# Full-height score products, query tiles loaded in pairs, DMA transposes of late x and a fixed order of tasks in a fused attention and SwiGLU kernel

## The chip, the core and the metric

The kernel runs on one core of one Trainium2 chip. The metric is the time on the device, in microseconds (us). Each run is one execution with its own time; one execution of each kernel was also profiled. "Span" is the length of the profiled execution, which lies about 1.7 us under the time of the same run (283.4 against 285.07 for the kernel before).

Engines: PE is TensorE (matrix products), PEld its weight loads, ACT is ScalarE, DVE is VectorE, POOL is GpSimd, SP issues DMAs.

## The reference, cut to what matters

```python
# q, k, v: (4, 8, 768, 64) f32; heads 0, 2, 6 see all earlier keys ("retrieval"),
# heads 1, 3, 4, 5, 7 only the first 4 keys and the last 64 ("sink + window")
scores = q @ k.T / 8                     # per batch and head, 768 x 768
scores = where(mask, scores, -1e9)       # causal, or causal & (sink | window)
a = softmax(scores)
x = (a @ v).transpose(0, 2, 1, 3).reshape(3072, 512)
g, val = x @ w_gate, x @ w_val           # 512 -> 1536
out = (silu(g) * val) @ w_out            # 1536 -> 512, f32
```

The kernel cuts the 3072 rows into 24 query tiles of 128. Two neighbouring tiles of a batch form a pair, 12 pairs in all, counted here from 0. Each pair has its own loads of q, k and v (512 KB each, f32). The three weight matrices (3.1 MB each) are loaded once, between the loads of pairs 1 and 4. A group of tiles, whose x is complete, goes through the gate, value and output products; a group's work is twelve column blocks of gate and value products and then its output products.

## The kernel before

q and k of a pair are cast to f16, transposed on TensorE, and copied from PSUM into one tensor `qkT`. Scores of a head use 64 rows of the array; the two heads of a head pair lie in the upper and lower half.

```python
SIZES = [2, 2, 4, 4, 4, 4, 4]            # query tiles per group
...
def transposes(n, w):                    # w: 0 for q, 1 for k
    tr = buf("tr", [128, 2, 4, 128], FH, "tr")
    for j in range(2):
        for p in range(4):
            nc.tensor.transpose(tr[:, j, p, :],
                hqs[n][:, w, j, p // 2, (p % 2) * 128:(p % 2 + 1) * 128], ident)
...
def scores(t, u, unit):
    sc = scs[t, u] = buf("sc", [128, 2, 4, 128], FP, "sc")
    for n in range(4):
        for s in range(2):               # the half of the rows, and of the PSUM tile
            if n < len(unit[s]):
                h, _, _, kk, vv = unit[s][n]
                nc.tensor.matmul(sc[:, s, n, :], kk,
                    T[s * 64:s * 64 + 64, 0, p, i * 128:(i + 1) * 128])
...
def xtranspose(t):                       # the attention's result, to feed the gates
    tr = buf("tr", [128, 4, 128], FH, "xtr")
    for p in range(4):
        nc.tensor.transpose(tr[:, p, :], xb[:, p].rearrange("p a d -> p (a d)"), ident)
```

A list scheduler with estimated durations orders the tasks while the kernel is built. At run time every engine works through its own list in order; the brackets in the timelines below name what an instruction waited for. An instruction that waits also holds back every later one of its engine.

The softmax here doesn't subtract the row's maximum and nothing guards it: scores larger than these inputs give would overflow.

## Time and profile before

| | kernel before |
|---|---|
| time, median of 3 runs | 285.65 us (284.93 to 286.28) |
| span of the profiled run | 283.4 us |
| PE busy | 261.6 us, 92% |
| copies, casts, masks: DVE, ACT, POOL busy | 161.5, 160.3, 133.7 us |
| end of the loads | about 105 us |

How to read it: PE is the bound as soon as it never waits, which holds from 90 us on (139.97 of the 140 us up to 230 are busy). What can be saved is therefore PE work, and the time that PE loses in the first 90 us. For the second I use one measure throughout. In the built order one can count the PE work that stands ahead of any instruction (0.2158, 0.1092, 0.0558 and 0.0295 us for products of 512, 256, 128 and 65 columns, from distances between starts; warm-up products count as nothing). The start of that instruction in the trace, less the work ahead of it, is the time lost up to there. The lines of the profile are shown in the prediction.

### The profile page before, as it was taken

What the parts mean: (1) busy time and instruction counts of PE and PEld (TensorE: products, weight loads), DVE (VectorE), ACT (ScalarE), POOL (GpSimd) and SP (SyncE); (2) the same over time, 40 slices, a digit from 0 to 9 for tenths busy, and PEclk for the clock granted to TensorE, in tenths of its full rate; (3) what the DMA queues carried; (4) which work ended last, traced back from release to release, by engine and by line L of the source; (5) the groups of instructions that cost most, each with busy time, mean ns of one, the idle gap of its engine ahead of it and who ended that gap; (6) DMA issues with size and microseconds to landing.
All of it is one profiled execution on the core that took longest, in us unless ns stands there. A gap on an engine that the chain in (4) does not pass through costs nothing.

```text
span 283.4 us, 5690 instructions
## 1 busy us (share of the span) xinstructions
PE 261.6 (92%) x2232; PEld 142.3 (50%) x2232; DVE 161.5 (57%) x319; ACT 160.3 (57%) x255; POOL 133.7 (47%) x194
## 2 busy tenths in 40 slices
PE   7358887989996999999999999999999999999994
PEld 6245665556644446454454454554554544444441
DVE  5374775646553667655574566685575564555500
ACT  3566877988954866648539656425526633332311
POOL 5669848876974557827425527408506410000000
PEclk9656999799999999999999999999999999999999
DMA  7999999999999990100000101110011010000022
GB/s 190 255 341 349 327 243 317 345 212 273 267 266 243 255 244 4 38 2 37 37 33 6 39 0 39 38 39 31 10 38 39 1 39 37 37 35 4 37 89 96
DMA packets 61514, 34.96 MB, mean 123 GB/s; under 512 B 26032, under 2 KB 57008, under 8 KB 61488
## 3 DMA queue, kind: packets, MB, share of 16 engines
q1 hardware_dynamic: 61344, 34.48, 45.0%
q8 instruction: 17, 0.28, 0.4%
q10 hardware_dynamic: 144, 0.13, 0.1%
q14 instruction: 9, 0.07, 0.1%
HBM read 28.31 MB, written 6.29 MB: 122 GB/s over the span
## 4 chain that ended last, share of the span: by engine, by line
PE 75%; DMA 13%; SPq 3%; ACT 2%; DVE 2%; issue 2%; POOL 1%; ACTq 0%; POOLq 0%
PE gv L635 39%; PE o_ps L665 18%; DMA raw<-in_k_dram 10%; PE sc L421 6%; PE av L463 5%; PE tr L355 3%; DMA raw<-in_v_dram 2%; PE xtr L480 2%; PE gv L665 2%; SPq L277 2%; SPq L269 1%; DMA raw<-in_moe_w_out_dram 1%; POOL e L454 1%; ACT e L435 1%; ACT hq L172 1%
## 5 line engine op out<-in xcount | busy, mean ns | idle before, releaser
L647 DVE SCALAR_TENSOR_TENSOR sil<-sig,gv 128x512 f32<-128x512 f32 (+1 forms) x84 | 51.1, 609 | 45.8 <-ACT sig L642 45.6
L635 PE MATMUL gv<-xt,wv_sb 128*128 128x512 f16 (+1 forms) x336 | 76.5, 353 | 0.7 <-DVE sil L647 0.7
L642 ACT ACTIVATE sig<-gv 128x512 f32<-128x512 f32 (+1 forms) x84 | 44.6, 538 | 55.9 <-PE gv L635 55.8
L635 PE MATMUL gv<-xt,wg_sb 128*128 128x512 f16 (+1 forms) x336 | 75.2, 352 | 0.0
L454 POOL TENSOR_TENSOR e<-e,m 128x1024 f16<-128x1024 f16 (+1 forms) x42 | 59.7, 1433 | 24.0 <-ACT e L435 23.6
L665 PE MATMUL o_ps<-wo_sb,h 128*128 128x512 f16 x264 | 67.6, 380 | 0.1
L435 ACT ACTIVATE e<-sc 128x1024 f16<-128x1024 f32 x48 | 49.2, 1025 | 23.1 <-PE sc L421 22.7
L654 DVE SCALAR_TENSOR_TENSOR h<-sil,gv 128x512 f16<-128x512 f32 (+1 forms) x84 | 51.2, 611 | 15.7 <-PE gv L635 12.1
L635 PEld LDWEIGHTS <-wg_sb 128*128 128x128 f16 x336 | 31.3, 99 | 26.3 <-issue 0.4
L665 PEld LDWEIGHTS <-h 128*128 128x128 f16 x288 | 27.2, 98 | 29.8 <-issue 0.4
L635 PEld LDWEIGHTS <-wv_sb 128*128 128x128 f16 x336 | 29.2, 99 | 23.8 <-issue 1.2
L454 POOL TENSOR_TENSOR e<-e,diag 128x128 f16<-128x128 f16 x60 | 24.8, 429 | 16.9 <-ACT e L439 11.3
L421 PE MATMUL sc<-qkT 64*128 64x128 f16 x392 | 26.9, 232 | 3.6 <-ACT e L435 2.3
L172 ACT CAST hq<-raw 128x512 f16<-128x512 f32 x44 | 25.9, 624 | 7.7 <-DMA raw<-in_q_dram 3.9
L463 PE MATMUL av<-vt,e 128*128 128x65 f16 x392 | 23.1, 197 | 5.8 <-POOL e L454 2.7
L421 PEld LDWEIGHTS <-qkT 64*128 64x128 f16 x392 | 14.8, 99 | 24.4 <-issue 19.1
L463 PEld LDWEIGHTS <-e 128*128 128x128 f16 x472 | 19.4, 99 | 13.9 <-POOL e L454 4.7
L471 DVE RECIPROCAL rc<-av 128x4 f32<-128x4 f32 x48 | 8.7, 181 | 26.0 <-PE av L463 25.7
L680 ACT COPY o_sb<-o_ps 128x512 f32<-128x512 f32 x22 | 12.9, 587 | 15.0 <-PE o_ps L665 15.0
L472 DVE TENSOR_TENSOR xb<-av,rc 128x256 f16<-128x256 f32 x48 | 20.4, 425 | 1.7
L174 DVE COPY qkT<-tr 128x1024 f16<-128x1024 f16 x14 | 17.1, 1222 | 7.2 <-PE tr L355 7.1
L378 POOL COPY k<-qkT 128x256 f16<-128x256 f16 x16 | 6.4, 397 | 30.7 <-DVE qkT L174 21.4
(50 smaller groups left out, 184.8 us busy)
## 6 DMA issues: line engine op xcount, KB each, us to landing
raw<-in_q_dram SPq DMA_DIRECT2D x12, 512.0 KB, 6.0
raw<-in_k_dram SPq DMA_DIRECT2D x12, 512.0 KB, 6.2
raw<-in_v_dram SPq DMA_DIRECT2D x24, 256.0 KB, 6.1
out_dram<-o_sb SPq DMA_DIRECT2D x23, 256.0 KB, 2.0
raw<-in_moe_w_gate_dram SPq DMA_DIRECT2D x6, 512.0 KB, 9.2
raw<-in_moe_w_val_dram SPq DMA_DIRECT2D x6, 512.0 KB, 8.9
raw<-in_moe_w_out_dram SPq DMA_DIRECT2D x6, 512.0 KB, 6.9
out_dram<-o_sb SPq DMA_DIRECT2D x1, 128.0 KB, 1.7
```

What stands on the lines that cost most here:

```text
L172: nc.scalar.copy(out=dst, in_=src)
L174: ENG[task.way[0]].tensor_copy(out=dst, in_=src)
L421: nc.tensor.matmul(sc[:, s, n, :], kk, T[s * 64:s * 64 + 64, 0, p, i * 128:(i + 1) * 128])
L435: nc.scalar.activation(out=e[:, :, 0:na], in_=sc[:, :, 0:na], func=AF.Exp, scale=scale)
L454: eng.tensor_tensor(out=ev, in0=ev, in1=mm, op=ALU.mult)
L463: nc.tensor.matmul(av[:, n, 0:65], ee, vv, start=(m == 0), stop=(m == len(bl) - 1))
L472: nc.vector.tensor_tensor(out=xbs[t][:, :, odd, :], in0=av[:, :, 0:64], in1=rc.to_broadcast([128, 4, 64]), op=ALU.mult)
L635: nc.tensor.matmul(ps, wsb[:, kk, j * 128:(j + 1) * 128], xt[:, kk, 0:w], start=(kk == 0), stop=(kk == 3))
L642: nc.scalar.activation(out=sg[g, j], in_=gs[g, j], func=AF.Tanh, scale=0.5)
L647: nc.vector.scalar_tensor_tensor(out=sl[g, j], in0=sg.pop((g, j)), scalar=1.0, op0=ALU.add, in1=gs.pop((g, j)), op1=ALU.mult)
L654: nc.vector.scalar_tensor_tensor(out=hs[g, j], in0=sl.pop((g, j)), scalar=0.5, op0=ALU.mult, in1=vs.pop((g, j)), op1=ALU.mult)
L665: nc.tensor.matmul(o_open[g, tt], hs[g, j][:, tt * 128:(tt + 1) * 128], wo_sb[:, j, :], start=(j == 0), stop=(j == NJ - 1))
```

## The change

Its intent is to fill the array's rows in the scores, to load and transpose q as pairs of tiles in a block-diagonal form, to take the transposes of late x off TensorE, and to replace the scheduler by a fixed order with 149 extra warm-up products in the early holes. The diff has 958 lines; this is its core, with cuts.

```diff
+ORDER = ("000403010205061F1G07xy1L1H1I1N1Mxm1O1Q1P08xt1R1J..."   # cut: the order of all tasks
+WAYS = ("0000000000000000000000000000000000000000000000..."       # cut: the engine of each
-    SIZES = [2, 2, 4, 4, 4, 4, 4]
+    SIZES = [4, 4, 4, 4, 4, 4]
+    HALVES = 4                          # column blocks of group 0 done in two halves of 256
+    XBAR = 12                           # tiles from 12 on: x by DMA transposes
...
-    qkT = [const.tile([128, 2, 4, S], FH, name=f"qkT{n}") for n in range(2)]
+    kT = [const.tile([128, 4, S], FH, name=f"kT{n}") for n in range(2)]
+    qT = [const.tile([128, 4, 2, 2, 128], FH, name=f"qT{n}") for n in range(2)]
+            nc.vector.memset(qT[n][0:64, :, 1], 0.0)       # zeros beside each head's q
+            nc.vector.memset(qT[n][64:128, :, 0], 0.0)
...
 def scores(t, u, unit):
+    for p, hh, c, kt in unit[0]:         # both heads of pair p in one product
+        nc.tensor.matmul(
+            sc[c // 4][:, c % 4:c % 4 + len(hh), :], block(t, p, kt),
+            qT[t // 2 % 2][:, p, hh[0]:hh[-1] + 1, :, half])
...
 def xtranspose(t):
+    if t >= XBAR:
+        for p in range(4):
+            nc.sync.dma_start_transpose(
+                out=xts[g][:, p, n * 128:(n + 1) * 128],
+                in_=xb[:, p].rearrange("p a d -> p (a d)"))
+        return
...
 def oevac(g, tt):                        # the last tile of the output
-        nc.scalar.copy(out=o_sb[:, 0:256], in_=o_ps[:, 0:256])
-        nc.vector.tensor_copy(out=o_sb[:, 256:512], in_=o_ps[:, 256:512])
+        nc.scalar.copy(out=o_sb[0:64], in_=o_ps[0:64])
+        nc.vector.tensor_copy(out=o_sb[64:128], in_=o_ps[64:128])
...
     for number in P.order():
+        if number < 3700:
+            P.tasks[number].run()
+        else:
+            warm(number - 3700)          # warm-up products between the tasks
```

The copy of transposed q out of PSUM becomes two copies of 64 partitions, since the two heads of a pair go to different places: one on ACT and one on DVE in nine of the twelve pairs, both on DVE in three.

## The prediction

> **What bounds the kernel now.** I read the busy table first, then the 40 slices, then the engines by stage, then the order of matmuls in time, and last the waits for loads.
>
> ```profile
> PE 261.6 (92%) x2232; PEld 142.3 (50%) x2232; DVE 161.5 (57%) x319; ACT 160.3 (57%) x255; POOL 133.7 (47%) x194
> ...
> PEclk9656999799999999999999999999999999999999
> DMA  7999999999999990100000101110011010000022
> ```
>
> TensorE is the only engine near full. Loads fill the DMA engines for the first 15 slices (some 105 us). The granted clock is low in slices 2 to 4 and in slice 8.
>
> ```profile
> 0.00:30.00 30.00, 19.48 (x195) 15.50 (x196) 16.56 (x38) 16.86 (x21) 21.39 (x42) 0.72 1.06 287
> 30.00:60.00 30.00, 26.52 (x287) 18.16 (x286) 20.00 (x48) 24.63 (x44) 21.93 (x30) 0.94 1.09 294
> 60.00:90.00 30.00, 26.02 (x310) 16.41 (x310) 16.05 (x39) 22.15 (x39) 21.50 (x33) 1.00 1.05 257
> 90.00:230.00 140.00, 139.97 (x1214) 69.87 (x1213) 86.81 (x161) 82.43 (x129) 68.91 (x90) 1.00 0.19 51
> ```
>
> The columns are stretch, length, busy PE, PEld, DVE, ACT, POOL, clock, DMA share, GB/s. From 90 us on TensorE never stops; before that it does. But busy time overstates, since neighbouring matmuls overlap in the record, so I count work by distances between starts in the dense part of the timeline: 0.216 us for a matmul of 512 columns (eight in 1.73), 0.109 for 256, 0.056 for 128 (eight transposes in 0.45), 0.0295 for 65. The scores are special:
>
> ```profile
> 102.18 1.90 PE L635 MATMUL gv<-xt,wg_sb 128*128 128x512 f16 x8
> 104.02 0.40 PE L421 MATMUL sc<-qkT 64*128 64x128 f16 x8
> 104.35 0.20 PE L463 MATMUL av<-vt,e 128*128 128x65 f16 x1
> ```
>
> Eight gate matmuls need 1.73 us, yet the scores start 1.84 after them: 0.11 is lost on entering. Eight score blocks go in pairs, one pair each 0.057, so 0.23; the next product starts after 0.33, so 0.10 is lost on leaving. A visit costs 0.21 us beside its work.
>
> Demand before, by the built order's counts: 768 of 512 columns 165.7, 192 of 256 20.9, 288 transposes 16.1, 472 value products 13.9, 472 score blocks 13.5, and 67 visits to scores 14.1: 244.2 us. Copying out and storing the last tile takes 3.7 (279.7 to 283.4). So 283.4 - 244.2 - 3.7 = 35.5 us are lost, nearly all early. Pair 4 of query tiles, counted from 0, shows why:
>
> ```profile
> 57.38 0.62 ACT L172 CAST hq<-raw 128x512 f16<-128x512 f32 x1 [0.46 <-DMA raw<-in_q_dram]
> 59.26 0.62 ACT L172 CAST hq<-raw 128x512 f16<-128x512 f32 x1 [0.71 <-DMA raw<-in_k_dram]
> ...
> 69.47 0.61 PE L355 MATMUL tr<-ident,hq 128*128 128x128 f16 x8
> ...
> 88.94 0.35 PE L463 MATMUL av<-vt,e 128*128 128x65 f16 x6 [2.13 <-POOL e L454]
> ```
>
> ACT waits for q and k of this pair; its k transposes run at 69.47, when about 40 us of demand are done (35.8 of work, some 20 visits). So 29.5 us were lost by then and 6.0 after it, 2.1 of them in the wait for a GpSimd mask at 88.94.
>
> [...] from 10 to 20 us the clock is 0.50, and eight score blocks that take 0.40 later are recorded with 0.61. [...] a DVE cast of 128x512 issued at 12.82, inside a POOL copy of 1.94 us, took 2.27 us, and 0.43 elsewhere. [...]
>
> **The change part by part.** Scores: 67 visits and 472 half-height blocks (27.6 us) become 196 full-height products of 256 columns (21.4) and 80 of 128 (4.5), since half of each moving operand is zeros. 25.9 instead of 27.6 saves only 1.7; a full unit of eight blocks costs 0.44 both ways.
>
> Late x: 12 tiles lose four PE transposes each, 48 x 0.056 = 2.7 us, and 12 DVE copies of 0.423. In the built order of the change the DMA transposes of a group's last tile stand 6 to 8 us of PE work ahead of the first gate, and all stand behind the input loads.
>
> Group sizes: seven groups become six, the first with halves for 4 of 12 column blocks. In 256-column form a gate pair keeps DVE 0.84 us for 0.87 of PE, in 512-column form 1.37 for 1.73, so the early stage loses a DVE limit. PE demand of the gates is unchanged.
>
> PE demand after: 832 x 0.216 = 179.5 (exact 0.2158), 64 x 0.109 = 7.0, 240 transposes 13.4, values 13.9, scores 25.9: **239.7**, less by 4.5. Extra warm-up products (189 for 40) stand in expected holes of the first 30 us and should keep the clock.
>
> Masks: POOL loses 85.0 us of them (46.8 + 24.8 + 13.4) and keeps some 18: about 4 x 2.13 + 7 x 1.33. It falls to some 70. DVE takes 20 of 0.68 and 13 of about 0.42, 23 casts of 0.43 and 11 output copies of about 0.69 (estimates scaled from rows of the same operation), and rises to about 195. ACT falls to about 143 (21 casts, 11 output copies, 4 weight casts fewer; about 9 us of q and k copies more). None passes TensorE.
>
> New order: this is the main term. The bytes ahead of k of pair 4 are the same (four pairs, all weights, its q), and DMA is full, so it should land near 59.3; a cast of 0.62 makes 59.9. In the changed order only 35.2 us of PE work stand ahead of its transposes (72 transposes, 24 for x, 49 + 15 score products, 97 value products, 64 gates of 256 columns, 64 products of 512). The PE cannot pass this point before 59.9, so at least 59.9 - 35.2 = **24.7** are lost. I choose this as the loss to that point, against 29.5 before: whatever the quicker start wins earlier is taken back by the load. The same test for k of pair 2 (cast at 38.2 before, 15.9 of work ahead) gives 22.9, consistent.
>
> Afterwards I keep 2.5 of the 6.0 lost: mask waits go, stores no longer stand between loads, but DVE gets tighter. Sum of span: 239.7 + 24.7 + 2.5 + 3.7 = 270.6; the timed median stands 2.2 above the profiled span (285.65 against 283.4): **272.8 us**, 4.5% faster.
>
> **The rivals.** (1) VectorE becomes the early bound. Between 10 and 60 us of PE demand it carries about 46 us by the counts, and the 2.27 us cast shows what a collision with GpSimd adds. For: 56 masks and casts move to it. Against: GpSimd's load halves. If it binds, 5 to 8 us more: 278 to 281. (2) The loads do go faster, as buffers come free sooner: slice 6 moved 243 GB/s where neighbours moved over 315, about 2 us of loading. Then 268 to 271. (3) DMA transposes and stores share one in-order queue with two output buffers; a transpose group over some 8 us would hold back gates or stores. No trace line gives their duration. Three late groups at a few us each: about 280. (4) The fixed order stalls every engine where one estimate was wrong, while it also keeps the slow clock: 3 to 5 us, 276 to 278.
>
> **Range and chances.** The low end, 266, needs a loss of 20 to pair 4 and almost none later; the high end, 279, one of rivals 1, 3 or 4 in full. The line for faster by over 2% is 279.9; only two rivals together pass it. So faster 0.88, same 0.10, slower 0.02.
>
> **What would show it.** Right: no 64-row matmuls; score units of eight blocks at 0.44 us without holes at their edges; PE waiting at the q or k transposes of pairs 2 to 4 for loads; the k transposes of pair 4 near 60 us; dense PE from some 65 us; POOL near 70 and DVE near 195 us; clock above 0.8 from 10 to 30 us. Wrong: k of pair 4 landing well before or after 59; PE waits on DVE in the middle; gates of the last three groups waiting on DMA transposes.

Marked cuts are passages that no trace or run of this case shows. The sum came to 239.7 + 24.7 + 2.5 + 3.7 + 2.2 = 272.8 us. That the DVE cast of 2.27 us was held up by the POOL copy running beside it is the reading of that one overlap; the 5 to 8 us of the first rival are an estimate.

## The result, and the profile after

| | before | changed |
|---|---|---|
| time, median of 4 runs | 285.49 us (284.93 to 286.28) | 277.46 us (276.55 to 278.45) |
| span of the profiled run | 283.4 us | 276.7 us |
| ratio | | 0.9717, 95% interval 0.9676 to 0.9759 |

A ratio is the mean time of one kernel's fast runs over that of the other's fast runs of the same rounds, so it is not quite the ratio of the medians quoted. The changed kernel is 2.8% faster. The profiled run of the changed kernel was its slowest of four.

First the page: busy times, then the granted clock and the DMA engines in 40 slices of 6.9 us.

```profile
PE 261.1 (94%) x2073; PEld 152.9 (55%) x2073; DVE 182.0 (66%) x368; ACT 146.5 (53%) x210; POOL 72.9 (26%) x106
...
PEclk9988989999999999999999999999999999999998
DMA  7999999999999994311022121122113021102233
```

ACT and POOL end near the prediction's 143 and 70 us; DVE, at 182, stays 13 us below its 195. The early clock is high (0.94 over the first 30 us, against 0.72), and the loads fill the DMA engines for as long as before (the first 15 slices, some 104 us here and 106 before).

The same stretches as before, columns as in the prediction:

```profile
0.00:30.00 30.00, 25.21 (x332) 22.23 (x333) 19.42 (x55) 18.22 (x24) 16.18 (x37) 0.94 1.02 277
30.00:60.00 30.00, 26.77 (x224) 16.88 (x223) 23.30 (x50) 21.40 (x34) 13.01 (x17) 0.94 1.07 298
60.00:90.00 30.00, 29.46 (x283) 18.59 (x280) 22.86 (x51) 23.39 (x33) 11.09 (x19) 1.00 1.10 252
90.00:230.00 140.00, 138.20 (x1052) 76.73 (x1051) 98.23 (x188) 72.27 (x104) 32.60 (x35) 1.00 0.30 67
```

PE now is dense from 60 us on, where it had 26.02 of 30 us before. In the first 30 us it is busier by 5.7 us, but 149 extra warm-up products of 0.056 us or more are in that. And the last stretch has 1.8 us of holes that the kernel before had not.

Then the timeline, at the places where PE falls behind (here and below, lines between those shown are left out):

```profile
37.87 0.76 DVE L179 CAST hq<-raw 128x512 f16<-128x512 f32 x2 [0.96 <-DMA raw<-in_q_dram]
38.36 0.73 PE L387 MATMUL tr<-ident,hq 128*128 128x128 f16 x8 [1.32 <-DVE hq L179]
...
63.21 0.61 PE L387 MATMUL tr<-ident,hq 128*128 128x128 f16 x8 [0.52 <-DVE qT L179]
...
111.66 1.17 POOL L179 CAST vt<-raw 128x512 f16<-128x512 f32 x2 [4.15 <-DMA raw<-in_v_dram]
112.79 2.12 POOL L495 TENSOR_TENSOR e<-e,m 128x1024 f16<-128x1024 f16 x1
114.97 0.42 PE L504 MATMUL av<-vt,e 128*128 128x65 f16 x8 [1.47 <-POOL e L495]
...
272.14 0.58 ACT L730 COPY o_sb<-gv 64x512 f32<-64x512 f32 x1 [2.00 <-PE gv L720]
272.75 0.69 DVE L731 COPY o_sb<-gv 64x512 f32<-64x512 f32 x1 [9.46 <-ACT o_sb L730]
```

The square brackets give the idle time of the engine before the line and what ended it. At 38.36 us PE waits for a cast of q of pair 2, which waited for its load: 13.7 us of work are ahead, so 24.7 us are lost here already, the loss that the prediction expected only at pair 4. At 63.21, the k transposes of pair 4, 35.2 us of work are ahead and 28.0 are lost, and the wait is not for k but for a DVE copy of q. At 114.97 a value product waits for a mask on POOL that stood behind the cast of a late v load. At the end the two half copies of the last tile run one after the other.

The span fell by 6.7 us: 4.5 us less PE work, 3.1 less lost (35.5 to 32.4), 0.9 more in the end from the first copy of the last tile on (3.7 to 4.6).

### The profile page after: what moved, and what is told of

Read it like the earlier page. It is cut to its first block, busy times and chain, and to the rows that moved or that the text cites. A ratio compares the mean times of both kernels' runs of the same rounds, so it can differ in the third digit from the quotient of the medians.

```text
span 276.7 us, 5346 instructions
## 1 busy us (share of the span) xinstructions
PE 261.1 (94%) x2073; PEld 152.9 (55%) x2073; DVE 182.0 (66%) x368; ACT 146.5 (53%) x210; POOL 72.9 (26%) x106
## 4 chain that ended last, share of the span: by engine, by line
PE 73%; DMA 8%; ACT 6%; SPq 4%; POOL 3%; issue 3%; DVE 2%; POOLq 0%; ACTq 0%; DVEq 0%
PE gv L692 37%; PE o_ps L720 17%; PE sc L470 8%; PE av L504 4%; DMA raw<-in_q_dram 3%; PE tr L387 3%; DMA raw<-in_k_dram 3%; PE gv L720 2%; ACT qT L177 1%; DMA xt<-xb 1%; ACT e L487 1%; SPq L524 1%; POOL e L495 1%; POOL vt L179 1%; SPq L304 1%
## 5 line engine op out<-in xcount | busy, mean ns | idle before, releaser
L487 ACT ACTIVATE e<-sc 128x1024 f16<-128x1024 f32 (+4 forms) x67 | 60.9, 910 | 37.3 <-PE sc L470 37.1
L709 DVE SCALAR_TENSOR_TENSOR h<-sil,gv 128x512 f16<-128x512 f32 (+1 forms) x76 | 49.3, 657 | 15.3 <-PE gv L692 13.7
L692 PEld LDWEIGHTS <-wg_sb 128*128 128x128 f16 x304 | 28.9, 99 | 27.3 <-issue 1.4
L470 PE MATMUL sc<-qT,kT 128*128 128x256 f16 (+1 forms) x228 | 35.9, 262 | 0.8 <-DVE kT L179 0.4
L495 POOL TENSOR_TENSOR e<-e,m 128x640 f16<-128x640 f16 (+1 forms) x11 | 18.2, 1662 | 42.6 <-ACT e L487 42.4
L470 PEld LDWEIGHTS <-kT 128*128 128x128 f16 x228 | 20.9, 99 | 12.1 <-issue 1.1
L179 POOL CAST vt<-raw 128x512 f16<-128x512 f32 x24 | 15.3, 659 | 41.5 <-DMA raw<-in_v_dram 37.4
L495 DVE TENSOR_TENSOR e<-e,m 128x1024 f16<-128x1024 f16 (+1 forms) x33 | 20.8, 631 | 7.6 <-ACT e L487 7.3
L387 PE MATMUL tr<-ident,hq 128*128 128x128 f16 x192 | 15.3, 223 | 3.8 <-DVE hq L179 3.0
L177 ACT CAST hq<-raw 128x512 f16<-128x512 f32 x23 | 14.0, 618 | 9.0 <-DMA raw<-in_k_dram 6.0
L387 PEld LDWEIGHTS <-hq 128*128 128x128 f16 x192 | 12.6, 100 | 8.4 <-DVE hq L179 3.6
L418 POOL COPY k<-kT 128x256 f16<-128x256 f16 x16 | 7.0, 435 | 37.9 <-DVE kT L179 24.8
```

The source lines that it names most:

```text
L179: ENG[task.way[0]].tensor_copy(out=dst, in_=src)
L387: nc.tensor.transpose(tr[:, j, p, :], hqs[n][:, w, j, p // 2, (p % 2) * 128:(p % 2 + 1) * 128], ident)
L470: nc.tensor.matmul(sc[c // 4][:, c % 4:c % 4 + len(hh), :], block(t, p, kt), qT[t // 2 % 2][:, p, hh[0]:hh[-1] + 1, :, half])
L487: nc.scalar.activation(out=e[:, 0:n], in_=whole_sc.pop((t, u))[:, 0:n], func=AF.Exp, scale=scale)
L495: ENG[task().way[0]].tensor_tensor(out=ev, in0=ev, in1=mm, op=ALU.mult)
L692: nc.tensor.matmul(ps, wsb[:, kk, j * 128:(j + 1) * 128], xt[:, kk, c[0]:c[1]], start=(kk == 0), stop=(kk == 3))
```

## The experiments

Most experiments alter only the lists. They are written as edits of the fixed order: ("after", a, b) puts the tasks b behind task a in the common order, from which each engine's list follows; ("way", n, t) gives task t to another engine of its choices. In the names, `cq2.0` is the first half cast of q of pair 2, `tr2.0` and `tr2.1` its q and k transposes, `evq`, `evk` the copies out of PSUM, `cx` a cast of v, `wc` the cast of a weight load, `gate0.5`, `tanh0.5`, `stt1 0.5`, `vals0.5`, `stt2 0.5` the steps of column block 5 in group 0. Built orders were checked for every dependence and every reuse of a buffer. Line numbers of the experiments are shifted against the changed kernel.

The runs, with the changed kernel itself as an anchor in the third call:

| call | run | median us (range) | ratio to before (95%) |
|---|---|---|---|
| 1 | half-height scores | 278.05 (277.42 to 279.60) | 0.9736 (0.9701 to 0.9770) |
| 1 | late x on TensorE | 281.29 (280.69 to 281.85) | 0.9842 (0.9811 to 0.9874) |
| 1 | few warm-up products | 276.88 (276.29 to 278.27) | 0.9695 (0.9660 to 0.9730) |
| 1 | transposes later | 278.63 (278.37 to 279.41) | 0.9756 (0.9722 to 0.9789) |
| 2 | weight casts on GpSimd | 278.40 (277.22 to 280.80) | 0.9732 (0.9687 to 0.9777) |
| 2 | mask first | 276.87 (275.46 to 277.44) | 0.9659 (0.9623 to 0.9694) |
| 2 | one copy of the last tile | 277.22 (276.58 to 278.30) | 0.9682 (0.9650 to 0.9715) |
| 2 | four edits | 275.80 (275.17 to 275.94) | 0.9627 (0.9597 to 0.9656) |
| 3 | changed kernel again | 277.53 (277.13 to 277.99) | 0.9683 (0.9643 to 0.9723) |
| 3 | both limits | 277.62 (277.13 to 279.08) | 0.9691 (0.9655 to 0.9728) |
| 3 | combined | 275.50 (275.16 to 276.68) | 0.9617 (0.9580 to 0.9655) |
| 4 | refined, five fast runs | 274.17 (273.72 to 276.98) | 0.9585 (0.9533 to 0.9636) |

A call is one set of runs taken together; the calls ran on different chips (6 for call 1, 5 for call 2, 11 for calls 3 and 4). For call 4 the kernel before was run only once more, and its other eleven runs are those of call 3. The kernel before gave medians of 285.13, 286.39, 286.85 and 286.87 in the four calls. The changed kernel's ratio came out as 0.9717 in the first set and as 0.9683 in call 3, with nearly the same median (277.46 and 277.53): it is the kernel before that scatters. So I compare medians of the edited kernels with 277.5 and take nothing under 1 us as shown by times alone. Calls 1 and 2 had no run of the changed kernel itself, so their comparison goes across chips. The mechanism is read from the traces, by the loss at fixed places:

| lost, us, up to | before | changed | later | GpSimd casts | both limits | combined | refined |
|---|---|---|---|---|---|---|---|
| k transposes of pair 2 | 24.0 | 24.5 | 24.8 | 26.0 | 22.4 | 22.1 | 21.6 |
| k transposes of pair 4 | 29.9 | 27.1 | 28.0 | 28.3 | 26.6 | 26.2 | 25.3 |
| copy of the last tile | 35.5 | 31.5 | 32.4 | 32.1 | 31.0 | 30.9 | 28.9 |

"Changed" is here the trace of the anchor run, whose time of 277.53 is the median; in the slower profiled run shown above the three numbers are 26.0, 28.0 and 32.4. A difference of 1 to 1.5 us between two traces of the same kernel is thus normal. The traces of mask first and one copy, whose early lists are those of the changed kernel, lie between these two: 24.9 and 24.9 at pair 2, 27.0 and 27.4 at pair 4.

### What the parts are worth: scores, DMA transposes, warm-up products

**Half-height scores.** The changed kernel with the old form; the two heads lie in different halves of the PSUM tile, as before. Query tiles with five key blocks use units of 7 and 2 score blocks in place of 8 and 1, so that no half has more than four.

```diff
-    for p, hh, c, kt in unit[0]:
-        nc.tensor.matmul(sc[c // 4][:, c % 4:c % 4 + len(hh), :], block(t, p, kt),
-                         qT[t // 2 % 2][:, p, hh[0]:hh[-1] + 1, :, half])
+    for n in range(len(rows[1])):
+        for s_ in range(2):              # rows[s_]: the blocks of one half of the rows
+            if n < len(rows[s_]):
+                p, kt = rows[s_][n]
+                part = slice(s_ * 64, s_ * 64 + 64)
+                nc.tensor.matmul(sc[s_][:, n if s_ else n + 4 - len(rows[0]), :],
+                                 block(t, p, kt)[part], qT[t // 2 % 2][part, p, s_, :, half])
```

> The changed kernel with the old form of the scores: each head's block is a product over 64 rows of the array[...]; order, copies, masks and loads stay as in the changed kernel. Theory (the demand account of the prediction): 472 half-height blocks and 68 visits cost 13.5 + 14.3 = 27.8 us where the full-height form costs 25.9, all of it on TensorE; so some 1.9 us more than the changed kernel (277.5), about 279.4, ratio to the kernel before near 0.978, and the 64-row units show gaps of some 0.1 us at both edges again. Rival (the form is the main part of the gain[...]): 283 or more, ratio over 0.99.

Measured: 278.05 us, 0.5 above the changed kernel; correct. From its timeline:

```profile
175.76 1.03 PE L768 MATMUL o_ps<-wo_sb,h 128*128 128x512 f16 x4
176.72 0.40 PE L507 MATMUL sc<-qT,kT 64*128 64x128 f16 x8
177.05 1.90 PE L740 MATMUL gv<-xt,wv_sb 128*128 128x512 f16 x8
```

Four products of 0.216 us end at 176.62, the scores start 0.10 later, and the next product comes after 0.33 us where eight half-height blocks need 0.23. So the edges are back, 0.20 us a unit of eight. But 0.10 + 0.33 is 0.43 us for eight blocks, and the full-height form takes four times 0.109, 0.44: for a full unit nothing is gained, only for the units with fewer blocks. Units that fill the two halves unevenly pay more on leaving (0.13 to 0.21 us in this trace). Summed over the 67 visits that is 27.8 us against 25.9 for the full-height form, a difference of 2.0, as the expectation had it; the times show only 0.5, within their scatter, and the trace loses some 1.6 us less elsewhere than the anchor's (0.9 of that is a wait of the anchor that comes and goes; see the end). The form of the scores is a small part of the gain; the rival of 283 or more is out.

**Late x on TensorE.** XBAR is 24, and the copies of late x are placed in DVE's list behind the next PE tasks.

```diff
-    XBAR = 12
+    XBAR = 24
+EDITS = [("after", "stt1 2.1.0", "xe12"), ("after", "sc14.0", "xe13"), ...]   # cut
```

> The changed kernel with x of the 12 late tiles transposed on TensorE and copied out by VectorE, as for the early tiles, in place of the DMA transposes. Theory: 48 transposes of 0.056 us come back to a TensorE that is full from some 65 us on, +2.7 us, less the one visible wait of 0.6 us for a DMA transpose: some 2 us more than the changed kernel, about 279.6, ratio near 0.979. Rival (the DMA transposes cost more than the trace shows, since they stand in the queue with the stores, or VectorE has holes that the copies fit badly): no difference or a little faster for the first half, ratio 0.972 or less; over 1 us beyond the theory's size (281 or more) if VectorE's 12 more copies of 0.42 us hold back the gates.

Measured: 281.29 us, 3.8 more, and beyond the expected 2. The demand rose by the counted 2.7 us; the rest is lost time (32.8 at the last copy against 31.5). The table of waits of PE shows two that are new; columns are the waiting group, the one waited for, us in total, times, and the longest:

```profile
PE xtr L584 <- DVE kT L233: 0.9, 1, 0.9
...
PE tr L441 <- DVE xt L589: 0.5, 1, 0.5
```

Transposes of x and of q and k share a single PSUM buffer, so x on TensorE also queues for it; the two waits stand at 177 and 187 us. Taking late x off TensorE is thus worth 3.8 us, more than the 2.7 that the products cost. This is the largest single part that I could isolate. The new order, the group sizes and the new division of masks and casts among the engines were not tested one by one; by the times, about 4 of the 8.0 us between the kernels remain with them together.

**Few warm-up products.** 131 of the 149 extra products are left out.

```diff
-        else:
+        elif number in (3718,):          # the first extra set, 18 products
             warm(number - 3700)
```

> The changed kernel without 131 of its 149 extra warm-up products (those placed in holes of the first 30 us; the 40 at the start and the first 18 stay). Theory: the loss of the early stage is set by when q and k of pairs 2 to 4 land, and TensorE waits for them at either clock, so the time stays within 1 us of the changed kernel (276.5 to 278.5), although the granted clock falls in slices 2 to 4. Rival (the quicker start is the clock's doing): with the clock near 0.5 to 0.65 in the first 30 us as in the kernel before, some 15 us of TensorE work take up to twice as long and the time rises by 3 us or more, 280.5 and over.

Measured: 276.88 us, 0.6 less than the changed kernel, although the granted clock read 0.7, 0.7 and 0.5 in slices 3 to 5, counted from 1 (14 to 34 us). The prediction was that the warm-up products "should keep the clock". They do (0.9 or more in each of these slices of the anchor), and it is worth nothing here, as PE waits at either clock: before the transposes of q and k it stood 2.1 us in this trace and 3.4 in the anchor's, before the scores 2.8 and 1.4. Something else was unexpected. Two traces in stretches of 1 us, of the kernel with all warm-up products (it is the one with one copy of the last tile):

```profile
15.00:16.00 1.00, 0.19 (x4) 0.02 (x1) 0.15 (x1) 0.35 (x2) 0.00 (x0) 1.00 0.95 155
16.00:17.00 1.00, 0.67 (x12) 0.57 (x13) 0.79 (x3) 0.98 (x2) 0.32 (x1) 1.00 0.58 127
```

and of the kernel with few:

```profile
15.00:16.00 1.00, 0.62 (x8) 0.45 (x9) 0.65 (x3) 0.97 (x3) 0.29 (x1) 1.00 1.42 246
16.00:17.00 1.00, 0.42 (x12) 0.33 (x10) 0.21 (x1) 0.98 (x2) 1.00 (x3) 1.00 1.00 295
```

The last number is GB/s. With all the warm-up products the loads dip, and k of pair 1 is cast from 15.85 us on, against 14.71 with few. The kernel with four edits, which also has few, shows no dip either. It is not scatter: in the traces with all warm-up products this load lands between 15.4 and 15.9 us, in these two with few at 14.46. Why the dip goes with the warm-up products was not found.

### Where PE's early loss comes from

**Transposes later.** My theory after the result: the lists put each pair's transposes ahead of ready gate and output work, so PE stops there until the load lands. The clock follows in the profiled run: it read 0.50 from 40 to 42 us, after the waits at 36.44 and 38.36, and eight gate products of 512 columns took 3.00 us from the first start to the next product's, where 1.73 is the time at the full clock.

```diff
+EDITS = [
+    ("after", "gate0.5.0", "cq2.0, cq2.1, tanh0.4.0, tanh0.5.0, tr2.0, ck2.0, evq2.1, evq2.0, ck2.1"),
+    ("after", "stt1 0.4.0", "tr2.1"),
+    ("after", "stt2 0.10.0", "tr4.0, ck4.1, ck4.0, evq4.0, evq4.1"),
+    ...                                  # cut: the same for pairs 3 and 4 to 7
+]
```

> The changed kernel with nothing but the order altered: casts, transposes and copies of q and k of pairs 2 to 7 stand later in every engine's list, behind gate and output products that are ready earlier. Theory (the loss of 28 us is made by lists that put each pair's transposes ahead of ready work, so that TensorE stops until the load lands and then runs at the lower clock): the stops at pair 2 (24.7 lost by 38.4 us in the changed kernel) and pair 4 (28.0 by 63.2 us) shrink, some 24 to 25 are lost by the time pair 4 is through, and the total falls by 3 to 4 us, to 273.5 to 274.5, ratio near 0.96. Rival (the rate of loading, or VectorE and ACT, bound this stage whatever the order): the stops move to other instructions and the time stays within 1 us of 277.5.

Measured: 278.63 us, 1.1 more, so the theory fell and its rival held (its limit was 1 us). The timeline of PE:

```profile
31.60 1.12 PE L738 MATMUL gv<-xt,wg_sb 128*128 128x256 f16 x8 [1.10 <-DVE sil L748]
...
36.90 0.60 PE L738 MATMUL gv<-xt,wv_sb 128*128 128x256 f16 x4 [0.95 <-DVE sil L748]
...
41.58 0.61 PE L433 MATMUL tr<-ident,hq 128*128 128x128 f16 x8 [0.96 <-ACT qT L223]
```

PE no longer waits for q of pair 2, but gates wait for a PSUM buffer that DVE's product frees. That product waited for a tanh on ACT, and ACT's list held a cast of value weights whose load had not landed until 29.76 us, ahead of it. DVE itself stood 0.7 us at such a cast before 36.4. So I formed a second theory: casts of late weight loads stand in ACT's and DVE's lists ahead of ready work.

**Weight casts on GpSimd.** POOL is busy for only 2 of the 10 us from 30 to 40 us.

```diff
+EDITS = [("way", 0, "wc v3"), ("way", 0, "wc v4"), ("way", 0, "wc v5"), ("way", 0, "wc g5")]
```

> The changed kernel with one thing altered: the casts of the four late gate and value weight loads (three on ACT, one on VectorE) are given to GpSimd, which is busy for only 2.0 of the 10 us from 30 to 40 us. Theory after the earlier runs (later transposes gained nothing, because ACT and VectorE stand in their in-order lists at casts whose loads have not landed, with ready tanh and product work behind them, so that TensorE waits for PSUM buffers of the gates): the waits of the gates for VectorE's products of about 0.4, 1.0 and 1.0 us between 28 and 38 us go, about 2 us less are lost by pair 2 and stay won: 275.5, ratio near 0.965. Rival (the q and k loads of pairs 2 and 4 bound the stage anyway, as the prediction had it): TensorE only arrives earlier at the transposes and waits there, the time stays within 0.7 us of the changed kernel, ratio 0.970 to 0.974. Second rival (GpSimd's casts hold back VectorE's copies): slower by 1 us or more.

Measured: 278.40 us, 0.9 more. The first rival was nearer. One line tells it:

```profile
38.64 0.73 PE L423 MATMUL tr<-ident,hq 128*128 128x128 f16 x8 [2.84 <-DVE hq L215]
```

PE got its gates done earlier and then waited 2.84 us for q of pair 2, which DVE cast when it had landed. It landed at 38.06 us in this trace and at 36.82 in the anchor's; the loads ran late from 23 us on, before the first of the moved casts (32.14), so 1.2 us of the wait is a difference between traces. The rest still fits the reading that two limits stood at the same place, and that each experiment had removed one. The next run tests it.

**Both limits.** GpSimd casts, and gates 4 to 6 ahead of the transposes of pair 2 in all lists.

```diff
+EDITS = [("way", 0, "wc v3"), ("way", 0, "wc v4"), ("way", 0, "wc v5"), ("way", 0, "wc g5"),
+    ("after", "stt2 0.3.256", "gate0.4.0, gate0.5.0, tanh0.4.0, tanh0.5.0, cq2.0, cq2.1, stt1 0.4.0, "
+        "vals0.4.0, tr2.0, ck2.0, evq2.1, vals0.5.0, stt1 0.5.0, evq2.0, stt2 0.4.0, ck2.1, "
+        "gate0.6.0, tr2.1, tanh0.6.0, stt2 0.5.0, evk2.0, stt1 0.6.0, vals0.6.0"),
+    ...                                  # cut: the tasks of tile 4 behind them
+]
```

> The changed kernel itself, built by the same means as the experiments with an empty list of edits, as the anchor for the other runs of this call: 277 to 278, ratio near 0.972.

The anchor gave 277.53 us.

> The changed kernel with two edits of the early stage together: the four weight casts on GpSimd (as in the run where TensorE then waited 2.8 us for the load of q of pair 2) and the gates 4, 5 and 6 of the first group ahead of the transposes of pair 2 in all lists (the earlier run of later transposes then waited 2.8 us for VectorE's products behind the weight casts). Theory: two limits stood at the same place within about a microsecond of each other, the load of q and the in-order weight casts, so that taking either away alone gains nothing; with both gone the loss by pair 2's k transposes falls from about 25 to about 23 us, and 1.5 to 2 us stay won: ratio about 0.966, near 275.5. Rival (a third limit, VectorE's and ACT's own work or the load of pair 4, takes it back by 65 us): ratio within 0.003 of the unedited kernel of this call.

Measured: 277.62 us, no gain in time, but the loss table shows what the theory said at its place: 22.4 us at the k transposes of pair 2, 2.1 less than the anchor. It also lies 2.1 below the lowest of the four traces with unaltered early lists. The rest of the theory failed: 2.0 us were lost again before the transposes of pair 3 at 47.11 us, where the anchor loses only 0.4 in that stretch, and at pair 4 only 0.6 of the gain was left, less than the spread of those four traces (27.0 to 28.0). So taking either limit away alone gained nothing, and with both gone the next chain took the gain. The anchor's timeline shows the chain at pair 4:

```profile
58.15 0.62 ACT L209 CAST hq<-raw 128x512 f16<-128x512 f32 x1 [0.81 <-DMA raw<-in_q_dram]
...
59.15 0.61 PE L419 MATMUL tr<-ident,hq 128*128 128x128 f16 x8
...
59.91 0.43 DVE L211 CAST hq<-raw 128x512 f16<-128x512 f32 x1 [0.73 <-DMA raw<-in_k_dram]
...
60.06 0.62 ACT L209 CAST hq<-raw 128x512 f16<-128x512 f32 x1
60.57 1.01 ACT L209 COPY qT<-tr 64x1024 f16<-64x1024 f16 x1
...
61.61 0.69 DVE L211 COPY qT<-tr 64x1024 f16<-64x1024 f16 x1 [0.87 <-ACT qT L209]
62.36 0.61 PE L419 MATMUL tr<-ident,hq 128*128 128x128 f16 x8 [0.67 <-DVE qT L211]
```

k of pair 4 is cast by 60.68 us, close to the prediction's 59.9. But its transposes start 1.7 us later: they need the one transposes buffer, which holds q until ACT has copied one half (behind an exponential and the cast of k) and then DVE the other. ACT and DVE do not overlap in it: DVE's copy waits 0.87 us for ACT's and starts at 61.61 us, when that is done (60.57 and 1.01). In the last tile of the profiled run it was the same (ACT from 272.14 for 0.58 us, DVE from 272.75). Why DVE waits for ACT there was not shown, and no run here shows the two side by side.

### Late waits

**Mask first.** One edit of POOL's list.

```diff
+EDITS = [("after", "mask13.0", "cx11.0, cx11.1")]
```

> The changed kernel with only GpSimd's list altered: the mask of tile 13 stands ahead of the casts of the last v load, instead of behind them. Theory: the 1.5 us wait of a value product for that mask near 115 us, and about 2 us of loss between 106 and 118 us in all, go; TensorE is dense from there on, so the time falls by about 1.5 to 2 us: 275.5 to 276, ratio 0.965 to 0.967. Rival (something else is just as late there): under 0.5 us.

Measured: 276.87 us, 0.6 less by the median, with a span of 273.7 in its fastest run. POOL's timeline:

```profile
110.16 2.13 POOL L528 TENSOR_TENSOR e<-e,m 128x1024 f16<-128x1024 f16 x1 [3.62 <-ACT e L520]
112.22 1.18 POOL L212 CAST vt<-raw 128x512 f16<-128x512 f32 x2
```

The mask starts 2.6 us earlier than in the profiled run of the changed kernel, and PE's wait for it is gone: between 105 and 115 us the loss grows by 0.3 us, against 1.7 in the anchor. The theory holds in the trace; the times, which scatter by 2 us, show less of it than expected. The v load was late in the first place because it stood in SP's in-order queue behind six output stores: in the profiled run of the changed kernel those were issued from 98.91 to 106.30 us, and it at 106.39.

**One copy of the last tile.**

```diff
-            nc.scalar.copy(out=o_sb[0:64], in_=o_ps[0:64])
-            nc.vector.tensor_copy(out=o_sb[64:128], in_=o_ps[64:128])
+            nc.scalar.copy(out=o_sb, in_=o_ps)
```

> The changed kernel with the last tile of the output copied by one ACT instruction of 128 partitions, instead of 64 partitions by ACT and then 64 by VectorE, which in the trace do not overlap (ACT 0.58 us, then VectorE 0.69 us). Theory: [...] the split only adds VectorE's 0.69 us: the tail falls from 4.8 to about 4.1 us, the time by 0.7 us. Rival (the two stores start more staggered now, and that hides the second copy): no difference, within 0.3 us.

Measured: 277.22 us, 0.3 less, too small for the times. In the trace the copy is one line:

```profile
271.39 0.58 ACT L762 COPY o_sb<-gv 128x512 f32<-128x512 f32 x1 [2.00 <-PE gv L752]
```

128 partitions take the same 0.58 us as 64 did on ACT, and DVE's half came after it (0.58 and then 0.69 us in the profiled run of the changed kernel), so the split only lost. The end, from this copy on, falls from 4.6 to 4.2 us, about half of the expected size: the last store is issued 0.5 us earlier (272.01 against 272.52) and then takes 0.3 us longer to finish (3.6 against 3.3). Why it does is not shown.

**Four edits.** GpSimd casts, mask first, one copy, few warm-up products.

> The changed kernel with four edits together: weight casts on GpSimd, the mask of tile 13 ahead of the last v casts, the last tile copied by one instruction, and only 58 warm-up products. Theory: the gains stand at different times on a TensorE that is otherwise dense, so they add: 2 + 1.8 + 0.7 + 0, about 273 us, ratio near 0.956. Rival (without the warm-up products the clock is low where the early waits are removed, so that the first gain is taken back): 275 or more.

Measured: 275.80 us, 1.7 less than the changed kernel, against 4.5 expected; the edits for late waits add up, the early one gives nothing, in line with the runs above. The rival's 275 or more holds as a number, but not for its reason: the early loss is no larger than the anchor's (24.0 and 26.3 us at pairs 2 and 4).

**Combined.** Both limits, mask first, one copy, few warm-up products, and the first gate weights loaded behind pair 1: ("after", "load x1", "load g0") and ("after", "ex2.0", "wc g0").

> The two edits of the run before, and with them: the mask of tile 13 ahead of the last v casts, one copy of the last tile, 58 warm-up products, and the first gate weights loaded after q, k and v of pair 1 instead of ahead of k. Theory: 1.8 us for the mask and 0.5 for the tail as measured, 1.5 to 2 for the early edits, and about 1 for the k of pair 1: 272.5 to 273.5, ratio near 0.954. Rival (the early gains are all taken back): ratio as with the four edits together before, 0.963.

Measured: 275.50 us. The rival held. A wait that took 0.39 us in the anchor had grown late, in ACT's timeline:

```profile
104.21 0.58 ACT L218 COPY o_sb<-o_ps 128x512 f32<-128x512 f32 x1 [1.40 <-DMA out_dram<-o_sb]
```

With two output buffers, a copy had to wait for a store that stood behind loads.

**Refined.** The combined version with these edits on top:

```diff
-    RINGS = {..., "osb": 2, ...}
+    RINGS = {..., "osb": 3, ...}
+    ("way", 1, "cq4.0"), ("way", 1, "ck4.1"), ("after", "xe5", "cq4.0"),
+    ("after", "tr4.0", "evq4.1, evq4.0, ck4.0, ck4.1"),
+    ("after", "out4.0.1", "gate5.0.0"),
+    # and vals0.7.0 ahead of val4.1 in the tasks of tile 4
```

> The combined version before, with what its trace still showed as waits taken up: a value column block ahead of the value products of tile 4 (0.5 us), q of pair 4 copied out before the second cast of its k, with two of pair 4's casts moved from ACT to VectorE (its k transposes ran at 61.43 us although k had landed at 59.1; they should run near 60.5), a third output buffer (0.8 us of an ACT copy waiting for a store near 104 us), and the first gate of the last group behind one more output product block (0.7 us). Theory: the loss at pair 4 is set by how fast q leaves the single transpose buffer, not by the load of k alone, so it falls from 26.2 to about 25 us and the total by 2 to 2.5 us: ratio about 0.954. Rival (each early gain is given back by the next chain in line, as in the runs before, and only the two late ones stay): about 1.3 us, ratio 0.957.

Measured: 274.17 us, ratio 0.9585; one of its six runs was slow (278.42) and is left out of both. At pair 4:

```profile
59.48 0.76 DVE L225 CAST hq<-raw 128x512 f16<-128x512 f32 x2
59.48 1.00 ACT L223 COPY qT<-tr 64x1024 f16<-64x1024 f16 x1 [1.89 <-DVE qT L225]
...
60.54 0.61 PE L433 MATMUL tr<-ident,hq 128*128 128x128 f16 x8 [0.61 <-ACT qT L223]
```

k of pair 4 is cast by 60.24 us; in the anchor 1.7 us passed from there to the transposes, here 0.3. The k transposes run at 60.54, where 60.5 was expected, and 25.3 us are lost there (25 expected). So it was indeed the way of q out of its buffer that held this place, not the landing of k alone. The total fell by 1.3 us, the size of the rival: most of the gain at pair 4 was again taken back by 80 us (26.9 lost in both kernels there), and the late edits stayed. This version is 3.3 us faster than the changed kernel and 4.1% faster than the kernel before, so it beats both.

## Why the prediction was right, and where its sizes were off

The time lies in the predicted range, 266 to 279 us. The mechanism held: PE work bounds the kernel from some 65 us on (29.46 of 30 us busy from 60 to 90, 138.20 of 140 from 90 to 230), and what is lost before is set around the loads of pairs 2 to 4. But the centre was 4.7 us too low, and the terms show where. The right column is the anchor run:

| term of the sum | predicted | measured |
|---|---|---|
| PE work | 239.7 | 239.7, counted; no holes at the scores |
| lost up to k of pair 4 | 24.7 | 27.1 |
| lost later | 2.5 | 4.4 |
| end | 3.7 | 4.6 |
| time above span | 2.2 | 1.7 |
| sum | 272.8 | 277.5 |

- **"I choose this as the loss to that point"** is the step that failed. 24.7 was a lower bound: k cannot be transposed before it has landed and been cast. I took the bound for the value. k was cast 0.8 us later than assumed (it landed at 59.9, not 59.3), and its transposes waited 1.7 more for q to leave the single transposes buffer; together 2.4. The refined kernel removed most of the second and stood at 25.3, near the bound.
- **"Whatever the quicker start wins earlier is taken back by the load"** held, more broadly than meant. At pair 2 the changed kernel has lost as much as the kernel before (24.5 against 24.0). An experiment that won 2.1 us there kept 0.6 at pair 4, and none of it could be seen in the time. It was not only the load that took it back, but also the next chain of ACT and DVE copies.
- **"Mask waits go, stores no longer stand between loads"** was wrong, and it is the larger part of the 1.9 us in "lost later": 1.7 us come from a mask behind a cast whose load stood behind six stores. Another 0.9 us is scatter: in the profiled run, the anchor and the combined version the very last DMA transpose landed 3.9 to 4.1 us after issue in place of 2.3, and PE lost 0.75 to 0.93 us on it at the gates of the last group; in eight other traces with DMA transposes it landed in time. In the refined kernel, which puts one more block of products ahead of that gate, it landed 4.0 us after issue and PE did not wait. After 80 us the refined kernel loses 1.9 us, the anchor 3.9.
- **The end** was kept at 3.7 us without looking at its new code: the two half copies of the last tile, now of 64 partitions each, take 0.58 and 0.69 us in turn, where column halves took 0.37 and 0.42.
- **Time above span** was taken from the median of one set and the span of a single run (285.65 and 283.4). The same run had 285.07.
- **Scores** were right in kind, and 1.7 us became 2.0 when the trace's visits are summed. **Late x** was counted at 2.7 us and is worth 3.8, as the shared buffer also comes free; the wait for the last DMA transpose, where it occurs, was in no step of the sum.

Of the rivals, the first half of the fourth is what happened: a fixed order in which engines stall where one estimate was off; its 276 to 278 us holds the result. Its second half, the clock, is worth nothing (276.88 us with few warm-up products against 277.5), so that its number fits is in part luck. VectorE as a bound (the first) shows only in waits behind other waits. The loads were not faster (the second): q of pair 2 was cast from 37.87 us on in the profiled run, against 36.34 before. A transpose group that holds back gates (the third) cost 0.9 us at most, not 7; the 1.7 us of the mask come from stores ahead of a load, some 7 us before the first DMA transposes were issued (106.39 and 113.53 us). How long they hold SP's queue was the number missing when this rival was weighed: four DMA transposes of 128x128 f16 (32 KB each) took 5.01 us to issue, two output stores of 128 KB 1.11, and both landed a median of 2.3 us after issue. The prediction's range had one slip: its own rivals 1 (up to 281) and 3 (about 280) each pass its high end of 279 and the line of 279.9, so "only two rivals together pass it" does not follow from its figures.

The loss that remains by pair 4, some 25 us in the best version, is not explained in full. About 20 us of it are there by 29 us, when little work is ready at all, and how much of that a different load order could win stays open.

## What to carry to other kernels

A lower bound from a load's landing is not yet an estimate: follow the whole way from landing to use, with each single buffer and each engine that frees it, and add what stands ahead in their lists. Where engines work through lists in order, a cast of a load that has not landed holds back everything behind it (here 4.15 us on POOL, and 1.47 on PE, which waited for the mask behind the cast), and when removing one wait gains nothing, look for a second that ends within a microsecond of it, and test both together (here even that moved most of the loss to the next chain). Late waits on a dense engine, on the other hand, add up: a mask behind a cast, a copy split over two engines, an output buffer too few were worth more here than any rearrangement of the early stage.
